# Four heads per K/V tile, products folded on TensorE, and a row-form MLP end in a one-token decode block

## The chip, the cores and the metric

The kernel runs on one core of a Trainium2 chip. The metric is device microseconds of one execution; smaller is better. Most executions of one kernel agree within 0.3%.

## The reference, cut to what matters

One token goes through pre-layernorm attention over a cache of 4096 keys and values (32 heads of 128, no sharing of heads), a residual, a second layernorm and a gated MLP (640 to 1728 to 640) with a residual.

```python
x = A_x                                                    # [1, 1, 640], bf16
q = layernorm(x) @ wq                                      # wq [640, 4096]: 32 heads of 128
scores = einsum("bhqd,bhkd->bhqk", q, k_cache) * 128**-0.5 # k_cache [1, 32, 4096, 128]
o = einsum("bhqk,bhkd->bhqd", softmax(scores), v_cache)
h = x + o.reshape(1, 1, 4096) @ wo                         # wo [4096, 640]
g, u = layernorm(h) @ w_gate, layernorm(h) @ w_up          # [640, 1728]
return h + (gelu(g) * u) @ w_down                          # [1728, 640]
```

Every weight and every K and V row is used once, so about 84 MB must come from HBM whatever the arithmetic looks like.

## The kernel before: the parts that matter

Each head's K and V is a tile of 128 partitions; a partition holds 32 consecutive keys, which is a run of 8 KB in HBM. K goes through the SyncE queue, most of V through the ScalarE queue. wq comes in three column pieces, so its runs are 1, 3 and 4 KB; wo comes in rows of 1280 B, because head h, element p sits on partition p.

```python
sp.dma_start(kbuf[:, h % NKB, :, :], A_k_cache[0, h, :, :].rearrange("(p g) d -> p g d", p=128))
...
sp.dma_start(wq_sb[:, :, 0:512], A_wq[:, 0:512].rearrange("(c p) n -> p c n", p=128))
... # K tiles 0 to 3
sp.dma_start(wq_sb[:, :, 512:2048], ...)
sp.dma_start(wq_sb[:, :, 2048:4096], ...)
...
sp.dma_start(wo_sb[:, :, :], A_wo[:, :].rearrange("(h p) n -> p h n", p=128))
```

VectorE multiplies K by a broadcast q and halves the products seven times; TensorE does P*V with one-column matmuls.

```python
prod = kbuf[h] * qb_sb[h]                    # 128x4096, L222
for w in [64, 32, 16, 8, 4, 2, 1]:           # L240; the last add writes sc, L236
    prod[..., 0:w] = prod[..., 0:w] + prod[..., w:2 * w]
...
for g in range(32):                          # L366
    matmul(ps_ot[:, 0:1], vbuf[:, h, g, :], p_sb[:, h, g:g + 1])
```

At the end, down is computed in column form (70 one-column matmuls, L405), the residual is added on VectorE (L306), five fp32 matmuls with the identity turn the columns into a row (L412), and the row is copied and stored.

The softmax here doesn't subtract the row's maximum and nothing guards it: scores larger than these inputs give would overflow.

## Time and profile before

| | before |
|---|---|
| time, median | 220.09 us (219.53 to 220.21, 3 runs) |
| span of the profiled execution | 217.9 us |
| HBM read | 84.23 MB |
| VectorE busy | 166.7 us |

The first fence is from the page of the kernel before: busy time of each engine, then three rows of the span cut in 40 slices (busy tenths of VectorE and of the 16 DMA engines, and GB/s), then two groups of instructions (count, busy us, mean ns, idle time before them and its releaser).

```profile
...
PE 70.8 (33%) x1490; PEld 49.2 (23%) x1490; DVE 166.7 (77%) x294; ACT 29.9 (14%) x145; POOL 0.5 (0%) x5
...
DVE  5189980791599999999999999999999999202201
...
DMA  4999999999999999999999999999999999999930
GB/s 128 408 417 408 415 422 423 423 418 418 421 418 426 408 390 415 426 423 418 424 418 424 414 426 415 424 420 426 414 423 417 412 373 390 364 400 409 377 116 3
...
L222 DVE TENSOR_TENSOR prod<-kbuf,qb_sb 128x4096 bf16<-128x4096 bf16 x32 | 71.9, 2288 | 20.3 <-DMA kbuf<-in_A_k_cache_dram 19.9
L240 DVE TENSOR_TENSOR prod<-prod 128x2048 bf16<-128x2048 bf16 (+2 forms) x192 | 83.5, 511 | 0.0
...
...
```

VectorE is at 9 of 10 from slice 12 to slice 34 and the DMA row reads 9 from slice 2 to slice 38. Two resources look full. A pair of heads takes VectorE 9.93 us (from one pair's first product to the next pair's, in the chain of waits) and the DMA 10.0 us (4.19 MB at 418 GB/s). They are balanced, so the arithmetic does not tell which one bounds; experiment 4 does. The second fence is the table of windows, 60 to 160 us; the last column is GB/s.

```profile
...
core 0: us, PE busy (x) PEld busy (x) DVE busy (x) ACT busy (x) POOL busy (x), PEclk, DMA share, GB/s
60.00:160.00 100.00, 28.46 (x668) 21.29 (x668) 99.66 (x161) 13.29 (x81) 0.00 (x0) 1.00 1.01 418
...
```

The third is the end of the chain of waits in order of time (start us, us, what). The profile lists an fp32 matmul twice, so the five of L412 read x10.

```profile
...
192.72 17.98 DMA wd_sb<-in_B_w_down_dram
...
210.84 2.02 PE pb L405 x70
...
213.10 2.30 PE pb L412 x10
...
215.43 0.68 DVE out_row L308
...
```

The last down weights land at 210.71 us, and 7.15 us of work follow.

### The profile page before, as it was taken

How to read it: one execution, taken by the hardware profiler on the slowest of the kernel's cores; microseconds unless marked ns; L12 is line 12 of the kernel's file. 1: busy time of each engine (PE TensorE's matmuls, PEld its weight loads, DVE VectorE, ACT ScalarE, POOL GpSimd, SP SyncE). 2: the span in 40 equal slices, each digit the busy share in tenths (PEclk: the TensorE clock that was granted, in tenths of full speed). 3: DMA queues.
4: the chain of work that ended last, by engine and by line, in shares of the span. 5: the costliest groups of instructions: out<-in, count | busy, mean ns of one | idle time of the engine just before them, and what ended most of it. 6: DMA issues, size and time to landing. Idle time of an engine off the chain costs nothing.

```text
span 217.9 us, 3679 instructions
## 1 busy us (share of the span) xinstructions
PE 70.8 (33%) x1490; PEld 49.2 (23%) x1490; DVE 166.7 (77%) x294; ACT 29.9 (14%) x145; POOL 0.5 (0%) x5
## 2 busy tenths in 40 slices
PE   0500872028606640422214040403203030435724
PEld 0100231024202230311213030302203030435722
DVE  5189980791599999999999999999999999202201
ACT  4300231001102230101101020201101010401100
POOL 0000000000000000000000000000000000000000
DMA  4999999999999999999999999999999999999930
GB/s 128 408 417 408 415 422 423 423 418 418 421 418 426 408 390 415 426 423 418 424 418 424 414 426 415 424 420 426 414 423 417 412 373 390 364 400 409 377 116 3
DMA packets 18389, 84.47 MB, mean 388 GB/s; under 512 B 1154, under 2 KB 7620, under 8 KB 10180
## 3 DMA queue, kind: packets, MB, share of 16 engines
q1 hardware_dynamic: 14340, 54.88, 63.0%
q10 hardware_dynamic: 4032, 29.36, 32.7%
q8 instruction: 12, 0.20, 0.4%
q14 instruction: 5, 0.04, 0.0%
HBM read 84.23 MB, written 0.00 MB: 387 GB/s over the span
## 4 chain that ended last, share of the span: by engine, by line
DVE 55%; DMA 27%; SPq 15%; PE 2%; issue 1%; DVEq 0%
DVE prod L222 27%; DVE prod L240 26%; DMA kbuf<-in_A_k_cache_dram 18%; SPq L149 11%; DMA wd_sb<-in_B_w_down_dram 8%; SPq L151 1%; DVE sc L236 1%; SPq L150 1%; PE pb L412 1%; PE pb L405 1%; SPq L124 0%; DVE out_row L308 0%; SPq L148 0%; SPq L134 0%; SPq L133 0%
## 5 line engine op out<-in xcount | busy, mean ns | idle before, releaser
L222 DVE TENSOR_TENSOR prod<-kbuf,qb_sb 128x4096 bf16<-128x4096 bf16 x32 | 71.9, 2288 | 20.3 <-DMA kbuf<-in_A_k_cache_dram 19.9
L240 DVE TENSOR_TENSOR prod<-prod 128x2048 bf16<-128x2048 bf16 (+2 forms) x192 | 83.5, 511 | 0.0
L366 PE MATMUL pb<-p_sb,vbuf 128*128 128x1 bf16 x1024 | 31.7, 166 | 112.2 <-ACT attnT_un L465 79.3
L366 PEld LDWEIGHTS pb<-p_sb,vbuf 128*128 128x128 bf16 x1024 | 29.5, 104 | 117.7 <-ACT p_sb L460 104.2
L338 PE MATMUL pb<-wq_sb,xlnT 128*1 128x512 bf16 x40 | 18.2, 624 | 10.6 <-DMA wq_sb<-in_A_wq_dram 10.3
L460 ACT ACTIVATE p_sb<-sc 128x32 bf16<-128x32 f32 x32 | 7.2, 226 | 85.0 <-DVE sc L236 84.8
L440 ACT ACTIVATE qb_sb<-pb 128x128 bf16<-128x128 f32 x32 | 8.4, 277 | 50.8 <-PE pb L347 50.8
L347 PE MATMUL pb<-q_row,ones_row_bf 1*128 1x128 bf16 x32 | 8.5, 283 | 1.9 <-ACT q_row L434 1.4
L338 PEld LDWEIGHTS pb<-wq_sb,xlnT 128*1 128x1 bf16 x40 | 3.9, 111 | 18.8 <-DMA wq_sb<-in_A_wq_dram 10.5
L256 DVE TENSOR_TENSOR hT_sb<-xT_sb,pb 128x5 f32<-128x5 f32 x1 | 0.2, 161 | 9.3 <-PE pb L380 9.3
L434 ACT CAST q_row<-pb 1x512 bf16<-1x512 f32 x8 | 4.6, 575 | 19.3 <-PE pb L338 19.2
L380 PE MATMUL pb<-attnN,wo_sb 128*128 128x1 bf16 x160 | 4.4, 165 | 5.5 <-DMA wo_sb<-in_A_wo_dram 5.5
L460 ACT ACTIVATION_READ_ACCUMULATOR p_sb<-sc 128x1 f32 x32 | 6.1, 190 | 0.1
L236 DVE TENSOR_TENSOR sc<-prod 128x32 f32<-128x32 bf16 x32 | 5.8, 223 | 0.0
L380 PEld LDWEIGHTS pb<-attnN,wo_sb 128*128 128x128 bf16 x160 | 4.4, 104 | 5.6 <-issue 5.6
L347 PEld LDWEIGHTS pb<-q_row,ones_row_bf 1*128 1x128 bf16 x32 | 3.1, 100 | 8.1 <-issue 5.1
L465 ACT COPY attnT_un<-pb 128x1 f32<-128x1 f32 x31 | 4.5, 146 | 2.6 <-PE pb L366 2.6
L306 DVE TENSOR_TENSOR outT_sb<-hT_sb,pb 128x5 f32<-128x5 f32 x1 | 0.2, 161 | 5.7 <-PE pb L405 5.7
L405 PE MATMUL pb<-hmT,wd_sb 128*128 128x1 bf16 x70 | 2.0, 165 | 3.9 <-DMA wd_sb<-in_B_w_down_dram 3.9
L391 PE MATMUL pb<-hlnT,wg_sb 128*128 128x1 bf16 x70 | 2.0, 165 | 2.8 <-DVE hlnT L275 2.8
L405 PEld LDWEIGHTS pb<-hmT,wd_sb 128*128 128x128 bf16 x70 | 2.0, 104 | 4.0 <-issue 4.0
L391 PEld LDWEIGHTS pb<-hlnT,wg_sb 128*128 128x128 bf16 x70 | 1.9, 104 | 2.9 <-DVE hlnT L275 2.9
(63 smaller groups left out, 26.1 us busy)
## 6 DMA issues: line engine op xcount, KB each, us to landing
kbuf<-in_A_k_cache_dram SPq DMA_DIRECT2D x32, 1024.0 KB, 11.2
vbuf<-in_A_v_cache_dram ACTq DMA_DIRECT2D x28, 1024.0 KB, 10.2
wo_sb<-in_A_wo_dram SPq DMA_DIRECT2D x1, 5120.0 KB, 32.8
vbuf<-in_A_v_cache_dram SPq DMA_DIRECT2D x4, 1024.0 KB, 25.9
wq_sb<-in_A_wq_dram SPq DMA_DIRECT2D x1, 2560.0 KB, 23.6
wg_sb<-in_B_w_gate_dram SPq DMA_DIRECT2D x1, 2160.0 KB, 37.7
wu_sb<-in_B_w_up_dram SPq DMA_DIRECT2D x1, 2160.0 KB, 18.2
wd_sb<-in_B_w_down_dram SPq DMA_DIRECT2D x1, 2080.0 KB, 19.7
```

Of the source, the lines that this page charges most:

```text
L149: sp.dma_start(wg_sb[:, :, 0:DF], B_w_gate[:, :].rearrange("(c p) n -> p c n", p=128)).then_inc(S("S_WG"), 16)
L222: inst = v.tensor_tensor(out=prod[:, par, :, :], in0=kbuf[:, h % NKB, :, :], in1=qb_sb[:, h % QR, :].unsqueeze(1).to_broadcast([128, G, DH ...
L236: inst = v.tensor_tensor(out=sc[:, h % 4, :], in0=prod[:, par, :, 0:1], in1=prod[:, par, :, 1:2], op=ALU.add)
L240: inst = v.tensor_tensor(out=prod[:, par, :, 0:w], in0=prod[:, par, :, 0:w], in1=prod[:, par, :, w:2 * w], op=ALU.add)
L338: ii = t.matmul(ps_q[j % 2][0:1, 0:512], xlnT[:, c:c + 1], wq_sb[:, c, j * 512:(j + 1) * 512], start=(c == 0), stop=(c == NC_D - 1))
L347: t.matmul(ps_qb[hh % 2][:, 0:DH], ones_row_bf[0:1, 0:128], q_row[0:1, hh * DH:(hh + 1) * DH], start=True, stop=True).then_inc(S("S_QB"), 1)
L366: inst = t.matmul(ps_ot[h % 2][:, 0:1], vbuf[:, h % NVB, g, :], p_sb[:, h % 4, g:g + 1], start=(g == 0), stop=(g == G - 1))
L380: inst = t.matmul(ps_projT[:, c:c + 1], wo_sb[:, h, c * 128:(c + 1) * 128], attnN[:, h:h + 1], start=(h == 0), stop=(h == H - 1))
L405: inst = t.matmul(ps_dT[:, c:c + 1], wd_sb[:, f, c * 128:(c + 1) * 128], hmT[:, f:f + 1], start=(f == 0), stop=(f == NCOL_F - 1))
L434: ii = a.copy(q_row[0:1, j * 512:(j + 1) * 512], ps_q[j % 2][0:1, 0:512])
L440: ii = a.activation(qb_sb[:, hh % QR, :], ps_qb[hh % 2][:, 0:DH], ACTF.Copy, scale=INV_SQRT_DH)
L460: inst = a.activation(p_sb[:, h % 4, :], sc[:, h % 4, :], ACTF.Exp, accum_out=RS[:, h:h + 1])
```

## The change

The intent: relieve VectorE. A tile now holds four heads, 32 partitions each, so a partition holds 128 consecutive keys (32 KB in HBM) and one tile is 4 MB. VectorE only multiplies; TensorE adds the products in 16 accumulating matmuls with the identity, each of 512 columns (64 keys of 8 elements), and VectorE reduces the last 8. Exp writes block-diagonal probabilities, so that one weight load of V serves four heads at once. q is projected in 32 equal rows per head and needs no broadcast step. The MLP ends in row form. With that the loads changed too: wq in runs of 16 and 24 KB, wo in one run of 40 KB per partition (the attention output is spread over partitions to match), everything through the SyncE queue. The diff is cut to its core, and long lines are abridged.

```diff
+    wq_v = A_wq[:, :].rearrange("(p c) n -> p c n", c=5)
+    d_wq = [P.dma("sync", wq_sb[:, 0:2, :], wq_v[:, 0:2, :]),
+            P.dma("sync", wq_sb[:, 2:5, :], wq_v[:, 2:5, :])]
+    def load_tile(n, *deps):
+        src = src[0, 4 * g:4 * g + 4, :, :].rearrange("h (p r) d -> (h p) (r d)", p=32)
+        landed[n] = P.dma("sync", slots[n % NSLOT][:, 0:128 * DH], src, *deps)   # 3 slots
 ... (cut)
-            for w in widths:                      # seven halving adds per head on VectorE
+            def fold(e, c=c):
+                for b in range(16):
+                    i = e.matmul(ps_f[c][:, :], id_b[:, :], prod[:, c, :, 8 * b:8 * b + 8],
+                                 start=(b == 0), stop=(b == 15))
+            reds[t] = V(lambda e, c=c: e.reduce_sum(sc[:, c, :], ps_f[c] as (g, 8), axis=AX.X), ...)
+            for j in range(4):                    # exp of head j into column j of p_bd
+                x = A(... e.activation(p_bd[32*j:32*j+32, G % 2, 64*c:64*c+64, j], sc[32*j:32*j+32, c, :], Exp, ...))
+            def pv(e, c=c, G=G, vt=vt):
+                for g in range(64 * c, 64 * c + 64):
+                    i = e.matmul(ps_o[:, 4 * G:4 * G + 4], vt[:, g, :], p_bd[:, G % 2, g, :], ...)
 ... (cut)
+    d_wo = P.dma("sync", arena[:, :], A_wo[:, :].rearrange("(p i) n -> p (i n)", i=32), qd)
 ... (cut: transpose and spread of the attention output, projection, layernorm, gate, up)
+    T(resid, c_idf, h)            # residual by 6 fp32 matmuls into the row, after up
+    def down(ms, last):
+                for b in range(2):
+                    i = e.matmul(ps_d[b][0:1, 0:320], hm[0:k, m:m + 1], wd_sb[0:k, m, 320*b:320*b+320], ...)
```

## The prediction

> **What bounds the kernel now.** The DMA. The page's DMA row reads 9 in slices 2 to 38, 84.23 MB are read from HBM, and windows of 5 us show 418 to 424 GB/s through the K/V stretch (48 to 180 us: 417). VectorE is 77% busy and the chain of waits names it for 55%, but it waits for K tiles at the start (19.9 us), and weights land back to back to 210.8 us; all compute after 187 us waits for weights (wo 5.5 us, wd 3.9 us). So VectorE's folding is nearly hidden already.
>
> **Removed.** The 192+32 halving adds on VectorE (83.5+5.8 us), 32 q broadcasts (8.5 us TensorE, 8.4 us ScalarE), 64 small K/V transfers, late activation table loads (2 x 1.28 us), the last transpose (2.29 us).
>
> **Added, per group of four heads.** Products 2 x 128x8192: 4 x 2.29 = 9.2 us VectorE. Folding: 32 matmuls of 512 columns; the trace's q projection has a start-to-start of 0.43 us for 512 columns, so at most 13.7 us. P*V: 128 weight loads at about 29 ns (64 in 1.87 us), 3.7 us. Two reductions of 512 PSUM values, about 0.7 us each (estimated from the 512-wide copy), eight small exps, about 3.3 us. A group's 8.4 MB take 20 us at 420 GB/s. Even with a slow clock TensorE needs 17.5 us, and VectorE's loop (first product 4.6, both folds 13.7, last reduction 0.7) 19 us. It fits, and three 4 MB slots keep transfers queued: the K/V part stays DMA-bound.
>
> **Where time moves.** (1) DMA start: the windows of 3 to 6 us show 230 to 279 GB/s (wq pieces of 1 KB rows); 8 KB rows save about 1.2 us. (2) wo as 40 KB runs instead of 1280 B rows: 175 to 190 us run at 362 to 380 GB/s; saves about 1.3 us. (3) wq and K/V as longer runs on one queue: 428 GB/s at 10 to 15 us against 419 later; saves about 2 us. Up weights then land at about 200.5 instead of 204.9 us. (4) End: before, from that landing to the end it is 13.0 us. After: up 2.0, residual 2.3 (fp32, as the old transpose), 28 row-form matmuls of 320 columns at 0.267 us = 7.5, copy 0.47, output DMA 1.6: about 14.0 us, now bound by TensorE and not by wd. The Trainium skill ("TensorE: Matmul & The Clock Gate", Part 1) says that TensorE runs at 1.2 GHz until about 3.4 us of sustained activity, then at 2.4; the trace's 0.43 us per 512 columns is the slow clock, even in a nearly always busy stretch (50.5 to 57.8 us) of one-column matmuls. So I expect a slow end (70%); a fast one would take 9 to 10.5 us.
>
> **Time.** Span about 214.5 with the slow end, 210.5 with the fast one; 2.2 us more in measured time. I predict 215.0 us, 8 in 10 within 211.0 to 219.5. Faster by over 2%: 0.58; within: 0.37; slower: 0.05.
>
> **What shows it.** K/V windows at 418 to 428 GB/s without gaps; VectorE busy down from 167 to about 90 us, TensorE up to some 150. The chain ends in DMA wd or wu, up, residual, down. Start-to-start of down matmuls 0.267 us (slow) or 0.136 (fast).
>
> **What would make it wrong.** Fold matmuls that read 8-element runs with a stride could stream slower than 0.43 us; above 0.47 the VectorE-TensorE loop passes 20 us per group and the kernel gets slower. One queue of 4 MB transfers could leave gaps. The q projection could delay the first K release by more than the 1.5 us I count, which the slots hide.

## The result, and the profile after

The kernel after takes 212.37 us (211.96 to 213.17, 4 runs) against 220.12 of before (4 runs, the three above and one more). The ratio is 0.966 (0.9634 to 0.9685). The profiled execution was the slowest of the four (213.17 us, span 211.4).

The page after, same rows as above, and the granted TensorE clock (PEclk, tenths of full speed):

```profile
...
PE 125.3 (59%) x1683; PEld 72.8 (34%) x1683; DVE 87.6 (41%) x66; ACT 31.7 (15%) x136; POOL 2.8 (1%) x10
...
DVE  2001295139416911972295159218720962102110
...
PEclk9999999965995599559659955995595569555558
DMA  6999999999999999999999999999999999899800
GB/s 242 443 443 446 409 453 434 403 474 415 394 478 412 409 465 415 414 453 422 425 440 422 431 437 415 446 434 406 447 434 419 440 402 490 348 418 380 301 23 0
...
L242 PE MATMUL bank<-prod,id_b 128*128 128x512 bf16 x256 | 73.0, 456 | 55.6 <-DVE prod L234 55.6
L234 DVE TENSOR_TENSOR prod<-slot,qb 128x8192 bf16<-128x8192 bf16 x16 | 70.1, 4422 | 44.7 <-DMA slot<-in_A_k_cache_dram 44.7
...
L265 PE MATMUL bank<-p_bd,slot 128*128 128x4 bf16 x1024 | 28.5, 165 | 8.1 <-ACT p_bd L254 8.1
...
```

VectorE's busy time fell by half, from 166.7 to 87.6 us, and the DMA row hardly changed: it still reads 9 or 8 until slice 38. What changed is the GB/s row. In the table of windows, 60 to 160 us:

```profile
...
60.00:160.00 100.00, 63.44 (x825) 35.55 (x822) 50.72 (x20) 18.95 (x88) 0.00 (x0) 0.74 1.00 430
...
```

430 GB/s against 418, at the same DMA share of 1.00. The end of the chain of waits:

```profile
...
152.50 33.42 DMA arena<-in_A_wo_dram
...
186.06 4.30 PE bank L310 x156
190.36 2.12 issue
192.47 0.28 PE bank L310 x4
...
195.53 3.70 PE bank L324 x121
199.23 1.04 issue
200.27 0.86 PE bank L324 x19
201.13 2.22 PE bank L334 x12
203.35 5.94 PE bank L353 x28
...
```

wo lands at 185.92 us, and the rest is one chain of TensorE and VectorE work; up weights (landed at 197.07) and down weights (202.68) are there before they are wanted. Twice TensorE stops with nothing to wait for: 2.12 us after 156 of the 160 weight-load and matmul pairs of the projection, and 1.04 us after 121 of the 140 pairs of gate and up. "issue" is the profile's word for that.

### The profile page after: what moved, and what is told of

Same layout as the page of the kernel before. It is cut to its first block, busy times and chain, and to the rows that moved or that the text cites. A ratio compares the mean times of both kernels' runs of the same rounds, so it can differ in the third digit from the quotient of the medians.

```text
span 211.4 us, 3675 instructions
## 1 busy us (share of the span) xinstructions
PE 125.3 (59%) x1683; PEld 72.8 (34%) x1683; DVE 87.6 (41%) x66; ACT 31.7 (15%) x136; POOL 2.8 (1%) x10
## 4 chain that ended last, share of the span: by engine, by line
DMA 58%; PE 24%; DVE 10%; issue 4%; ACT 3%; SPq 1%
DMA slot<-in_A_k_cache_dram 42%; DMA arena<-in_A_wo_dram 16%; PE bank L242 13%; DVE prod L234 8%; PE bank L353 3%; PE bank L265 3%; ACT p_bd L254 2%; PE bank L310 2%; PE bank L324 2%; PE bank L334 1%; DVE sc L250 1%; SPq L50 1%; PE bank L198 0%; DVE out_row L359 0%; ACT ln L202 0%
## 5 line engine op out<-in xcount | busy, mean ns | idle before, releaser
L242 PE MATMUL bank<-prod,id_b 128*128 128x512 bf16 x256 | 73.0, 456 | 55.6 <-DVE prod L234 55.6
L234 DVE TENSOR_TENSOR prod<-slot,qb 128x8192 bf16<-128x8192 bf16 x16 | 70.1, 4422 | 44.7 <-DMA slot<-in_A_k_cache_dram 44.7
L242 PEld LDWEIGHTS bank<-prod,id_b 128*128 128x128 bf16 x256 | 28.3, 114 | 97.8 <-DVE prod L234 57.1
L254 ACT ACTIVATE p_bd<-sc,zero_t 32x64 bf16<-32x64 f32 x64 | 27.7, 433 | 133.4 <-DVE sc L250 132.7
L265 PE MATMUL bank<-p_bd,slot 128*128 128x4 bf16 x1024 | 28.5, 165 | 8.1 <-ACT p_bd L254 8.1
L265 PEld LDWEIGHTS bank<-p_bd,slot 128*128 128x128 bf16 x1024 | 27.8, 97 | 10.7 <-ACT p_bd L254 8.8
L250 DVE TENSOR_REDUCE sc<-bank 128x64 f32<-128x512 f32 x16 | 11.1, 692 | 33.6 <-PE bank L242 33.6
L254 ACT ACTIVATION_READ_ACCUMULATOR p_bd<-sc,zero_t 32x1 f32 x64 | 11.8, 184 | 0.0
L218 PE MATMUL bank<-arena,xlnB 128*32 128x512 bf16 x40 | 4.7, 628 | 9.8 <-DMA arena<-in_A_wq_dram 9.8
L353 PE MATMUL bank<-slot,hm 128*1 128x320 bf16 (+1 forms) x28 | 6.0, 388 | 0.0
## 6 DMA issues: line engine op xcount, KB each, us to landing
arena<-in_A_wq_dram SPq DMA_DIRECT2D x1, 3072.0 KB, 14.3
```

The source lines that it names most:

```text
L218: i = e.matmul(ps_q[hf][32 * j:32 * j + 32, :], xlnB[:, c, :], wq_j[:, c, j, 4 * hf:4 * hf + 4, :], start=(c == 0), stop=(c == 4))
L234: m = V(lambda e, c=c, G=G, kt=kt: e.tensor_tensor(out=prod[:, c, :, :], in0=kt[:, 64 * c:64 * c + 64, :], in1=qb[:, G, :].unsqueeze(1).to ...
L242: i = e.matmul(ps_f[c][:, :], id_b[:, :], prod[:, c, :, 8 * b:8 * b + 8], start=(b == 0), stop=(b == 15))
L250: reds[t] = V(lambda e, c=c: e.reduce_sum(sc[:, c, :], ps_f[c][:, :].rearrange("p (g d) -> p g d", d=8), axis=AX.X), folds[t], exps.get(t ...
L254: x = A(lambda e, c=c, j=j, G=G: e.activation(p_bd[32 * j:32 * j + 32, G % 2, 64 * c:64 * c + 64, j], sc[32 * j:32 * j + 32, c, :], ACTF.E ...
L265: i = e.matmul(ps_o[:, 4 * G:4 * G + 4], vt[:, g, :], p_bd[:, G % 2, g, :], start=(g == 0), stop=(g == 127))
```

## Experiments

Two theories stand against each other. **R (runs):** the DMA bounds both kernels, and the gain comes from longer runs per partition. **V (VectorE):** the gain comes from the relief of VectorE, which held the K buffers. Then there is the end, which the change made longer: what it costs, and why TensorE stops.

### 1. K/V in 8 KB runs again

```diff
-        landed[n] = P.dma("sync", slots[n % NSLOT][:, 0:128 * DH], src, *deps)
+        landed[n] = [P.dma("sync", slots[n % NSLOT][:, 4096*q:4096*q+4096], src[:, 4096*q:4096*q+4096], *deps)
+                     for q in range(4)]
```

> The kernel after the change, with each 4 MB K/V tile loaded by four transfers of 8 KB per partition instead of one of 32 KB: the run length of before, nothing else. Theory R (longer runs per partition move more bytes per second and that is most of the gain in the K/V stretch): a group of K and V, 19.45 us between landings in the kernel after, becomes about 19.95 us (before: 417 GB/s), wo lands 3 to 4 us later, and the time rises from 212.4 to about 216 us. Rival V (the gain comes from VectorE no longer holding the K buffers): no change, within 0.7 us of 212.4.

Measured: 216.45 us, ratio 0.986 (0.9841 to 0.9878), so about 4.4 us slower than the kernel after (0.020 of 219.5). The two ratios come from different rounds, and each is known to 0.2 to 0.3%, so such a difference is good to about 0.7 us. The landing of wo is a steadier mark: in the kernel after and the six runs below that keep its K/V, wq and wo loads it is 185.7 to 186.1 us. Here wo landed at 189.38 us, 3.5 later than the 185.92 of the kernel after. The table of windows of this run:

```profile
...
60.00:160.00 100.00, 61.03 (x804) 34.79 (x803) 50.72 (x20) 17.52 (x82) 0.00 (x0) 0.74 1.01 420
...
```

420 GB/s: the rate of before is back, although VectorE is as idle as after. In the traces an 8 KB packet takes a DMA engine 312 ns (median) and a 32 KB packet 1214 ns: four of the small ones take 2.8% longer, which is the difference between 418 and 430. Theory R holds for K/V. All transfers still go through one queue, and 420 is close to the 418 of the two queues before, so the queues do not make the difference. The run changes the length of the runs and the number of transfers together; the packet times speak for the runs. A straight line through the two medians (an estimate: 11 ns per packet and 37.6 ns per KB) gives 58 ns for 1280 B and 1515 ns for 40 KB; the medians measured in the trace of the kernel after are 56 and 1518. So each packet costs a fixed 11 ns or so, whatever its length, and short runs pay it more often.

### 2. wo in rows of 1280 B again

```diff
-    d_wo = P.dma("sync", arena[:, :], A_wo[:, :].rearrange("(p i) n -> p (i n)", i=32), qd)
+    d_wo = P.dma("sync", wo_sb, A_wo[:, :].rearrange("(h p) n -> p h n", p=128), qd)
     (the transpose and spread of the attention output left out, attnN used directly)
```

> The kernel after the change, with wo loaded in 1280 B rows as before and the attention output used without the spreading step. Theory R: one DMA engine moves 1280 B packets at 21.1 GB/s and 40 KB packets at 26.8 (read from the packets of the two traces), so wo takes 15.5 us instead of 12.5, lands 3 us later, and since the end hangs on the landing of wo, the time rises by about 3 us to 215.4. My prediction's step 2 gave it 1.3 us, to 213.7. Rival (the packets are slow only because they share engines with others): under 1 us.

Measured: 213.74 us, ratio 0.9725, about 1.4 us slower. wo landed at 188.38 us, 2.5 later, close to theory R's 3. The time was not: it came to the 213.7 of my prediction's step 2 and not to theory R's 215.4. The 2.1 us stop within the projection was gone: with five matmuls fewer before it, it fell into the layernorm and took 0.98 us. Up then waited for its own weights, which landed at 199.56 instead of 197.07, and 0.54 us of the second stop were left. That is a first hint about the stops.

### 3. wq in column pieces again

```diff
-    d_wq = [P.dma("sync", wq_sb[:, 0:2, :], wq_v[:, 0:2, :]), P.dma("sync", wq_sb[:, 2:5, :], wq_v[:, 2:5, :])]
+    d_wq = [P.dma("sync", wq_sb[:, :, lo:hi], wq_v[:, :, lo:hi]) for lo, hi in ((0, 512), (512, 2048), (2048, 4096))]
```

> The kernel after the change, with wq loaded in the column pieces of before (runs of 1, 3 and 4 KB) instead of 16 and 24 KB. Theory R: the first K tile lands 1.2 to 1.7 us later (25.3 us in the kernel after), all later landings shift by as much, and the time rises by as much, to about 213.9. If the q projection mattered, the shift of the end would be larger than that of the first K landing.

Measured: 213.81 us, ratio 0.9734, about 1.6 us slower. wo landed at 187.52 us instead of 185.92. From the chain of waits of this run:

```profile
...
154.39 33.14 DMA arena<-in_A_wo_dram
...
```

As theory R expected. The first K tile landed at 27.09 us instead of 25.30, but that mark is loose: in the runs of experiments 6 to 11, which load wq as the kernel after does, it lies between 25.4 and 26.5. The edit also makes the q projection wait for all of wq at once, but the delay is there before that can matter: the last piece of wq landed at 17.38 us instead of 15.59.

### 4. The kernel before with most of VectorE's folding taken away

```diff
-            widths = [64, 32, 16, 8, 4, 2, 1]
+            widths = [16, 1]
```

> The kernel before the change with two of its seven halving adds per head left (a wrong result on purpose): VectorE needs 2.9 instead of 5.0 us per head. Theory R (the kernel before is bound by the DMA): the time stays within 1 us of 220.1. Rival V (VectorE's folding bounds it): VectorE's work between 57 and 187 us shrinks by some 40 us and the time falls by 4 us or more.

Measured: 219.35 us, ratio 0.9989 (0.9974 to 1.0004). The scores are wrong; the comparison with the reference passed all the same, so it does not see errors in the attention of this block, in any kernel of this document. Engines' busy time, VectorE's row and the clock row of its page:

```profile
...
PE 71.0 (33%) x1490; PEld 49.3 (23%) x1490; DVE 95.3 (44%) x134; ACT 29.9 (14%) x145; POOL 0.5 (0%) x5
...
DVE  5179200630458292745547291827456373002201
...
PEclk9999996555555555555555555555555555555555
...
```

VectorE's busy time fell from 166.7 to 95.3 us, and the time by a tenth of a per cent, which is within the noise. Rival V is out: VectorE did not bound the kernel before.

### 5. All three old load forms at once

The edits of experiments 1 to 3 together.

> The kernel after the change with all three old load forms at once: K/V in 8 KB runs, wo in 1280 B rows, wq in column pieces. What is left of the change is its arithmetic: folding on TensorE, block-diagonal probabilities, the new q projection and end. Theory R (the gain is made of run lengths): the three single losses, 4.4, 1.4 and 1.6 us, nearly add up, to 219.5 to 221 us, the time of the kernel before, although VectorE is busy for half as long. If the arithmetic is worth something by itself, the time stays below 218.

Measured: 220.02 us, ratio 1.0007 (0.9961 to 1.0053). The windows of 60 to 160 us:

```profile
...
60.00:160.00 100.00, 62.78 (x804) 35.37 (x803) 50.72 (x20) 17.91 (x83) 0.00 (x0) 0.73 1.01 421
...
```

With the old runs, the new arithmetic is as fast as the old one, within half a per cent (1 us). The three single losses (4.4 + 1.4 + 1.6 = 7.4 us) make up the whole gain of 7.6 us (1.0007 - 0.966 of 219.5), within their noise. The zero is a sum: in the traces the last weights land at 210.08 us instead of 210.71, and the work after that takes 8.5 us instead of 7.2, with both stops in the chain before it (1.91 and 1.01 us).

### 6. and 7. The stops: 64 and 128 useless matmuls

The Trainium skill ("Runtime: NRT & Kernel Launch", Instruction fetch mechanics) says that instructions are fetched in blocks of 16 KiB, 256 instructions, by a DMA queue, the next block while the current one runs, and that crossing a border is mostly hidden. The trace agrees with the block: the page lists 13 packets and 0.21 MB on an instruction queue, 16 KB each. It does not agree with "hidden" for two of the borders: such a transfer ran from 189.99 to 191.05 us and another from 197.70 to 198.82, and TensorE went on 1.4 us after each. The stops are 127 pairs apart by the trace (4 of the projection, 2 of the layernorm, 121 of gate and up; with 128 useless matmuls 4, 2 and 122), and 128 pairs are 256 instructions.

```diff
+    def pad(e):
+        for k in range(64):          # 128 in the second run
+            i = e.matmul(ps_z[:, 200:201], id_b[:, :], ones_b[:, 0:1], start=True, stop=True)
+    T(pad, c_idb, c_onesb)           # while TensorE waits for the first K tile
```

> The kernel after the change, with 64 useless one-column matmuls (64 weight loads, 64 matmuls) on TensorE while it waits for the first K tile. In the kernel after, TensorE stops for 2.1 us within the projection (after 156 of 160 weight-load and matmul pairs) and for 1.0 us within gate/up (after 121 of 140), waiting for nothing the trace names; each time a 16 KB instruction-queue transfer ended 1.4 us before it went on, and the two stops are 128 pairs apart. Theory F (TensorE runs out of instructions at the border of a 256-instruction block): borders move by 64 pairs, to pair 92 of the projection and pair 57 of gate/up, each with time for the fetch before; both stops vanish or fall under 0.5 us in sum, and the time falls by 2 to 3 us, to about 209.5 to 210.5. Rival D (the stops are late data, weights still in flight): no change, within 0.7 us of 212.4.

> As the run with 64 useless matmuls, with 128 of them: a whole block. Theory F: the borders fall where they fell in the kernel after, the stops come back after pair 156 and pair 121, 2.1 and 1.0 us long, and the time is that of the kernel after, 212.4, within 0.7 us. If more idle-time work on TensorE as such were what helped, this one would be as fast as or faster than the one with 64.

Measured: with 64, 210.30 us, ratio 0.9566, about 2.1 us faster than the kernel after; with 128, 212.45 us, ratio 0.967, the kernel after again. First TensorE's timeline with 64 (start, busy us; projection, gate, up), then the chain with 128:

```profile
...
186.19 4.41 PE L316 MATMUL bank<-aP,arena 128*128 128x1 bf16 x160 [2.57 <-DMA arena<-in_A_wo_dram]
...
193.39 2.25 PE L330 MATMUL bank<-hlnT,slot 128*128 128x1 bf16 x70 [1.49 <-DVE hlnT L321]
197.25 2.25 PE L330 MATMUL bank<-hlnT,slot 128*128 128x1 bf16 x70 [1.61 <-DMA slot<-in_B_w_up_dram]
...
```

```profile
...
185.83 4.30 PE bank L316 x156
190.12 2.19 issue
192.31 0.26 PE bank L316 x4
...
195.34 3.73 PE bank L330 x122
199.07 1.02 issue
200.09 0.86 PE bank L330 x18
...
```

With 64 the 160 projection pairs run through, and so do gate and up. With 128 both stops are back at the same pairs (up to one). So the stops are borders of instruction blocks. The gain is less than the 3.2 us of the two stops, because now up waits for its weights (1.61 us, until 197.20). Not all of it is the stops: between the traces with 128 and with 64, up ends 1.45 us earlier (199.50 instead of 200.95), and down takes 4.46 us instead of 4.94, because the clock rose earlier within it. What is left open: when a fetch is asked for. From its start to TensorE going on it took about 2.5 us, and a block of weight-load and matmul pairs at 27.6 ns runs out in 3.5 us; the fetches started late for a reason that the trace does not name.

### 8. The residual before gate and up

```diff
+    T(resid, c_idf, h)
     ga = T(glu(ps_g, wg_sb), hl, d_wg)
     up = T(glu(ps_u, wu_sb), d_wu)
-    T(resid, c_idf, h)
```

> The kernel after the change, with the residual's matmuls (2.29 us) placed before gate and up, in the 1.5 us in which TensorE waits for the second layernorm, instead of after them. The end hangs on TensorE's order of work: down starts 1.3 to 1.5 us earlier, gate 0.8 us later; the time falls by about 1.4 us, to 211.0. If the end hung on the landing of the last weights (202.7 us), it would stay.

Measured: 210.88 us, ratio 0.9602, 1.3 us faster. The end of its chain:

```profile
...
184.46 16.67 DMA slot<-in_B_w_down_dram
...
201.26 5.73 PE bank L353 x28
...
```

Down starts at 201.26 instead of 203.35 us, as soon as the first down weights are there. TensorE's timeline shows one more thing, gate and up:

```profile
...
195.91 4.42 PE L324 MATMUL bank<-hlnT,slot 128*128 128x1 bf16 x140
...
```

All 140 pairs run through: the second stop is gone too. The instruction block of that border was fetched from 196.17 us on, 0.3 after gate began, and in the kernel after only 2.2 after it (197.70). So the 1.3 us are the gain of the new order together with a lost stop of 1.04 us, and what the order alone is worth is not shown. Down's earlier start, 2.1 us where 1.3 to 1.5 were expected, says the same.

### 9. The end of the MLP in column form again

```diff
-    T(resid, c_idf, h)                 (and the row-form down, its two copies)
+    dn = T(down, g9, *d_wd)            # 70 one-column matmuls
+    oT = V(lambda e: e.tensor_add(g_t[:, 0:5], hT[:, :], ps_q[0][:, 0:5]), dn)
+    tn = T(turn, oT, c_idf)            # five fp32 matmuls with the identity
+    o1 = V(... out_row[0:1, 0:512] ...); o2 = A(... out_row[0:1, 512:640] ...)
```

> The kernel after the change with the end of the MLP in the column form of before: 70 one-column matmuls for down, the residual added on VectorE, five fp32 transposes, copies; no residual matmuls. My prediction held the row form for 1 us slower than the old end, with the slow clock. Theory: down in column form ends 2.1 us after the landing of wd (202.7), then 0.2, 2.3, 0.7 and 1.6 us: the end is at 209.6 instead of 211.4 in the trace, the time about 210.6. If the row form is worth having, the time rises instead.

Measured: 212.29 us, ratio 0.966: the same as the kernel after. I expected 1.8 us less. From the timeline of this run:

```profile
...
203.04 2.81 PE L345 MATMUL bank<-hm,slot 128*128 128x1 bf16 x70 [2.28 <-DMA slot<-in_B_w_down_dram]
...
206.11 2.29 PE L354 MATMUL bank<-id_f,g_t 128*1 128x128 f32 x10 [0.25 <-DVE g_t L349]
...
208.44 0.68 DVE L357 CAST out_row<-bank 1x512 bf16<-1x512 f32 x1 [2.39 <-PE bank L354]
...
```

Down started at 203.04 us as expected, but its 70 pairs took 2.81 us where the kernel before needed 2.02. The trace shows where the 0.8 us went. All 70 pairs of the kernel before are 128 x 128, because it fills the last weight block up with zeros. This run, like the kernel after, has no filling, and five of its pairs have 64 rows (the weight loads of L345: ns min/median/max, first and last start, forms):

```profile
...
L345 PEld LDWEIGHTS bank<-hm,slot x70: 102/104/115, 203.0 to 205.7; 128*128 128x128 bf16 x65, 64*128 64x128 bf16 x5
...
```

Pairs start 27 ns apart, but around each 64-row pair three intervals in a row are 98, 116 and 46 ns, 0.18 us more than three usual ones (at the last pair there is only the first of them). So this is not quite the end of before. And I had set my figure against the profiled run of the kernel after, which was 0.8 us slower than its median. The row form as written is as fast as this column form; a column form with filled weights was not run.

### 10. A version that beats both

The 64 useless matmuls, the residual early, and down in four column groups: hm is spread over 32 equal columns, and four matmuls of 160 columns go to four quarters of the array.

```diff
+    g9 = V(... hm[:, :, :] = gu * t1, each broadcast to 32 columns ...)
-                for b in range(2):
-                    i = e.matmul(ps_d[b][0:1, 0:320], hm[0:k, m:m+1], wd_sb[0:k, m, 320*b:320*b+320], ...)
+                for j in range(4):
+                    i = e.matmul(ps_d[32*j:32*j+32, 0:160], hm[0:k, m, :], wd_sb[0:k, m, 160*j:160*j+160], ...)
+    o1 = V(lambda e: e.tensor_copy(out_sb[:, :], ps_d[:, 0:160]), dn)
+    d_out = P.dma("sync", out as 4 rows of 160, out_sb[0:128:32, :], o1)
```

> A version meant to beat both: the kernel after with 64 useless matmuls at the start (no stop at block borders), the residual before gate/up, and down with hm spread over 32 columns in four column groups of 160 outputs, as the q projection does it (four matmuls of 512 columns took 0.43 us there). Then the last landing of wd (202.8 us) should bound the end: 0.14 to the first matmul, about 0.7 for the last four blocks, 0.3 copy, 1.7 output: 205.7 to 206.0 in the trace, 207.5 us in time (ratio about 0.945). If column groups do not run side by side here, down takes 7.5 us with the slow clock and the time is 212 or more.

Measured: 207.83 us, ratio 0.9453 (0.9422 to 0.9483). TensorE's timeline (gate, up, down) and the end of the chain:

```profile
...
193.46 2.25 PE L332 MATMUL bank<-hlnT,slot 128*128 128x1 bf16 x70 [0.80 <-DVE hlnT L323]
197.03 2.25 PE L332 MATMUL bank<-hlnT,slot 128*128 128x1 bf16 x70 [1.32 <-DMA slot<-in_B_w_up_dram]
201.24 2.31 PE L366 MATMUL bank<-slot,hm 64*32 64x160 bf16 x56 [1.96 <-DMA slot<-in_B_w_down_dram]
```

```profile
...
184.67 16.44 DMA slot<-in_B_w_down_dram
...
201.24 2.34 PE bank L366 x53
...
```

The Trainium skill ("TensorEngine Tiling (Array Packing)", Theoretical Speedup) gives up to four times for 32 columns. Here 56 matmuls of 160 columns, which one by one at 1.2 GHz would take 7.5 us (an estimate: 56 x 160 / 1.2 GHz), took 2.31 us, part of it waiting for the last weights. The granted clock was 0.5 during down, and in the steady part four matmuls start every 0.13 us, the time of one such matmul at that clock (160 / 1.2 GHz): the trace agrees. The end is bound by the landing of wd again, as in the kernel before.

### 11. The down weights in long runs too

```diff
-    wd_v = B_w_down[0:1664, :].rearrange("(c p) n -> p c n", p=128)
+    wd_v = B_w_down[0:1664, :].rearrange("(p c) n -> p c n", p=128)
-    ... w[:, c, m * 128:m * 128 + k] ...                  # weight columns of gate and up
+    ... w[:, c, m:1664:13] (m < 13), w[:, c, 1664:1728] ...
```

> The version with the tiled end, with the down weights also loaded as long runs: 13 consecutive rows per partition (11.5 and 5 KB) instead of 1280 B rows, for which gate and up read their weight columns with a step of 13. Theory R: 1280 B packets go at 21.1 GB/s per DMA engine, runs of 5 KB and more at 25 or better, so the last 2.1 MB land 1.0 to 1.2 us earlier (202.8 us in the run with the tiled end) and the time falls from 207.8 to about 206.8. Against it: if weight loads with a step are slower than 29 to 32 ns per pair, up ends later than wd lands and the gain is lost or turned round; at twice the time up ends at 201.5 and the time is about 208.

Measured: 209.68 us, ratio 0.9541, 1.9 us slower than experiment 10. TensorE's timeline (gate and up, down):

```profile
...
193.22 8.81 PE L333 MATMUL bank<-hlnT,slot 128*128 128x1 bf16 x140 [0.80 <-DVE hlnT L323]
203.31 2.18 PE L367 MATMUL bank<-slot,hm 64*32 64x160 bf16 x56 [1.28 <-DVE hm L359]
```

The 140 pairs of gate and up took 8.81 us, 63 ns each, against 2.25 us for 70 (32 ns) in experiment 10. A weight load that reads its columns with a step of 13 takes twice the time, the case that the expectation had named as the risk. The last weights landed only 0.3 us earlier (202.46 instead of 202.78), not 1.0 to 1.2. The long run must not be paid for with stepped weight loads.

## Why the prediction was right, point by point

- **"The DMA bounds the kernel; VectorE's folding is nearly hidden."** Right. Experiment 4 takes 71 us of VectorE work away and gains 0.1%, within the noise; experiment 5 keeps the new arithmetic and gains nothing.
- **"It fits; three 4 MB slots keep transfers queued."** Right. The DMA share is 1.00 from 60 to 160 us, and VectorE's products wait for nothing but their own K tiles (44.7 us). The folds streamed faster than I feared: 256 of them keep TensorE busy for 73.0 us, about 9 us per group against the 13.7 at most. The Trainium skill ("TensorE: Matmul & The Clock Gate", Part 1) has the clock at 1.2 GHz until some 3.4 us of activity. In the folds the traces come near it: the first fold matmuls start 0.43 us apart, and 3.5 us after the first one, at 33.3 us, they become twice as fast; over the eleven traces with the new folds this took 3.2 to 5.5 us. At the end the trace of the kernel after does not agree: TensorE works without a gap from 200.27 us, and the clock rises at 207.4, 7.1 us later. In experiments 9 to 11 it does not rise at the end at all. Why is open.
- **(1) DMA start, 1.2 us.** Experiment 3: 1.6 us, which holds the share of wq in term (3) too.
- **(2) wo, 1.3 us.** Experiment 2: wo lands 2.5 us later without the change, and the time moves by 1.4 us, the rest hidden by a stop that went away.
- **(3) K/V and wq as longer runs, 2 us.** This is the term that was mis-sized most. K/V alone is worth 3.5 us of landing and 4.4 us of time (experiment 1). I had read 428 GB/s from one window of 5 us and counted 2 us; at 428 instead of 419 the 67 MB of K/V would already give 3.4 us, and the measured rate was a steady 430 over the whole K/V stretch. In landings the three terms are worth 1.6 + 2.5 + 3.5 = 7.6 us where I had counted 4.5. So up weights landed at 197.07 us, not at 200.5.
- **(4) The end, about 14.0 us from the landing of the up weights.** Measured 14.3 us in the profiled run, but made of other parts: two stops of 3.2 us that I had not foreseen, so that up ended 4.1 us after its weights landed and not 2.0, and down in 5.94 us instead of 7.5, because the clock rose at 207.4 us. That the size came out right is luck: two errors, one up and one down, cancelled.
- **Sum.** 215.0 predicted, 212.4 measured, within the range: the mechanism was right and the gain of long runs was under-estimated, by 3 us in the landings.

## What to carry to other kernels

Where the DMA row is full, look at the length of the runs before the arithmetic: here 8 KB against 32 KB per partition was worth 2.8% of the K/V time, and relief of the busiest engine was worth nothing that could be measured. After such a gain, look at the chain after the last landings again: an order of work, instruction-block borders and matmuls whose stationary operand had one column cost 4.5 us there (212.37 - 207.83). A border can be moved with useless instructions in idle time, if the profile shows a stop that waits for nothing.

## What the Trainium skill lacked or had wrong

- "DMA: Bandwidth & Descriptors", Specifications, puts the least transfer for line rate at 512 B. Here one DMA engine moved packets of 1280 B at 21.2 GB/s, 3456 B at 25.2, 8 KB at 26.1 and 32 KB at 26.9 (mean time of a packet in experiments 1 and 2), and the step from 8 to 32 KB alone was worth about 4.4 us of the kernel's time.
- "Runtime: NRT & Kernel Launch", Instruction fetch mechanics, calls the cost of a block border mostly hidden. Here two borders stopped TensorE for 2.1 and 1.0 us on the chain, in streams of weight-load and matmul pairs of 27.6 ns.
- "TensorE: Matmul & The Clock Gate", Weight-path perf modes, gives the range of column steps that a fast weight load allows, and no cost of a step; the page on SBUF speaks of a penalty for wide steps, without its size for a weight load. Here a step of 13 took 63 ns per pair instead of 32.
- "TensorE: Matmul & The Clock Gate", Part 1, warns that the clock events of a trace can be unreliable, but not that they can be missing altogether: the kernel before shows a clock of 1.00 throughout, and the same TensorE work in experiment 4 shows 0.58 on average, while its 512-column matmuls start 0.43 us apart, at 1.2 GHz, in the trace of before. Other executions of the same kernel show 0.573 to 0.578.
